# Attention, experts and FFN on one core: second product of expert blocks two and three from seven block products, interleaved with the first

## The chip, the cores and the metric

One core of one Trainium2 chip runs the whole program. The metric is the device time of one execution in microseconds (us). A product of matrices runs on TensorE (PE in the profile; PEld is its weight load), element-wise work on VectorE (DVE), ScalarE (ACT) and GpSimd (POOL); SyncE (SP) issues the DMAs. On-chip data lie in SBUF, TensorE's results in PSUM banks.

## What is computed

```python
x = attention(q, k, v)                 # 4 batches x 8 heads x 576 x 64, window 128, ALiBi -> x: 2304 x 512
P = exp(x @ w_gate - max); 8 x { P /= P.sum(1); P /= P.sum(0); P *= N / E }     # 2304 x 8
out = 0
for e in range(8):                     # experts, D = 512, F = 1024
    h = np.maximum(x @ w1[e], 0.0)     # "first product"
    out += P[:, e:e+1] * (h @ w2[e])   # "second product"
h = out @ w_in                         # FFN, 512 -> 2048
result = (h * np.cos(h)) @ w_out       # 2304 x 512
```

Everything is float32; a product of two float32 matrices is made of three products of parts (high x high, high x low, low x high).

## The kernel before

After the attention (the first 195 us) the tokens go through in three blocks of 768 (TB; half of it, HB, is 384, and TPB = 6 tiles of 128). Six phases follow each other: expert blocks ("moe", 0), ("moe", 1), ("moe", 2), which the text calls blocks one to three, then the same for the FFN. A phase runs over **units** of 256 hidden columns: NU1 = 32 units in an expert block (UPE = 4 for each expert), NU2 = 8 in an FFN block, 120 in all.

**First product of a unit** (`product`, L773). It is made from seven block products (a Strassen-Winograd scheme: 2 x 2 blocks with 7 products in place of 8), numbered m, each of six matmuls 128x384 (L766). Activations come from the seven tiles xtT../xtB.. that `stages` (POOL, L267) and `combos` (ACT L293, DVE L294) make once for a phase, weights from `wa` (1,792 KB). The main loop's order is `for m in (5, 1, 4, 2, 3, 6, 0, 7)`: product 4 is that of the unit before, and m = 0 stands for a **batch**. Products 1, 6, 7 and 4 add up in one PSUM bank y (two buffers), 5 and 3 in z, 2 in x; between them ACT copies the bank as it stands (`keep`, L796), and DVE adds copy and bank (L799). ReLU and the split into high and low part follow (ACT L722, DVE L723); in an FFN phase `cos_chain` (L732 to L755) does that, on ACT, DVE and POOL.

**Second product** (`batch`, `g2`, L870 to L872): 36 matmuls 128x512 for the unit before: six token tiles, each with two halves of the 256 columns and three part products. `evac` takes each of the six banks out on DVE and adds it, times the weight P of the token, to `acc_moe` (L861). Tokens are the rows of this sum. The FFN wants it the other way round, so ahead of each FFN phase `x2_pieces` turns it with 24 transposes on TensorE (L713), three to a step, and ACT copies (L716).

**Weights.** During block one the raw weights of a unit are loaded, the sums of the scheme (`prep_s`, POOL L120) and the split (`prep_a`: ACT L129, DVE L132; `prep_b`: ACT L143, POOL L145) are made, and the result is stored to HBM (wd1, wd2). Blocks two and three load it again: `wa` from wd1 with the load of unit n+1 issued behind product 4 of unit n-1 (L109, by SP), and `wb` (1,024 KB) from wd2 in the batch. Both have two buffers.

**Background.** `slot()` runs one step of each list of generators; slots lie between the products and in the batch. Among the generators is `convert_f64`: the FFN's weights come as 64-bit floats, and DVE converts them in 32 chunks of seven operations (L218 to L238), one chunk for a unit, in blocks two and three. `prep_ffn` (POOL L120 and L181, ACT L179) makes the sums and splits of the eight FFN units from them.

The order on each engine is the order of the code; each engine works off its own queue, and semaphores hold it where data is not there.

## Time and profile before

| what | value |
|---|---|
| median of three runs | 2098.69 us (2096.76 to 2104.01) |
| the profiled execution | 2100.89 us, of it span 2099.1 us |
| PE, DVE, ACT, POOL busy | 98%, 65%, 36%, 23% of the span |
| chain of work that ended last, by engine | PE 92%, DVE 4%, ACT 1%, issue 1% |
| DMA | 457 MB, mean 218 GB/s |

Busy time is the time in which an engine's instructions ran; the chain is followed back from the last instruction to what released it. Where PE is nearly always busy and nearly the whole chain, the length of PE's queue is the time, and the few gaps in it come on top. The page's rows stand further below.

### The profile page before, as it was taken

The numbers are of one execution on the slowest core, as the hardware profiler recorded it, in microseconds if no ns is written. First come the engines' busy times: TensorE is split into PE (matmuls) and PEld (weight loads), VectorE is DVE, ScalarE is ACT, GpSimd is POOL, SyncE is SP. The second block draws the span as 40 slices with busy tenths as digits, with TensorE's granted clock in tenths as the row PEclk, the third lists the DMA queues.
The fourth block names the chain that finished last, engine by engine and source line by source line (L and its number), as shares of the span: only waits on it lengthen the run. The fifth ranks groups of instructions, "written<-read, shape, count | busy, mean of one in ns | idle before, by whom it ended". The sixth has DMA issues, their size and how long they took to land.

```text
span 2099.1 us, 28328 instructions
## 1 busy us (share of the span) xinstructions
PE 2059.7 (98%) x10623; PEld 1821.5 (87%) x10623; DVE 1366.0 (65%) x2473; ACT 765.0 (36%) x1544; POOL 491.4 (23%) x524
## 2 busy tenths in 40 slices
PE   8989999999999999999999999999999999999998
PEld 6657889999899899899899899998998988899897
DVE  5665876666667677777776676555545565856765
ACT  6775433333333212222222322222221245454443
POOL 4343334333333002112113212110000113224222
PEclk9989999999999999999999999999999999999999
DMA  5633667767776568888888687675454454465552
GB/s 143 164 77 92 213 238 260 261 239 266 252 252 248 200 223 290 289 283 298 279 292 281 212 273 271 223 243 193 177 199 176 172 181 178 166 219 185 208 182 110
DMA packets 162106, 456.96 MB, mean 218 GB/s; under 512 B 67504, under 2 KB 106416, under 8 KB 131248
## 3 DMA queue, kind: packets, MB, share of 16 engines
q1 hardware_dynamic: 161968, 455.15, 63.2%
q8 instruction: 83, 1.36, 0.3%
q14 instruction: 55, 0.45, 0.1%
HBM read 326.65 MB, written 128.45 MB: 217 GB/s over the span
## 4 chain that ended last, share of the span: by engine, by line
PE 92%; DVE 4%; ACT 1%; issue 1%; POOL 0%; DMA 0%; POOLq 0%; DVEq 0%; ACTq 0%
PE y_moe L766 18%; PE g_moe L871 12%; PE g_moe L872 12%; PE g_moe L870 12%; PE z_moe L766 9%; PE x_moe L766 5%; PE y_ffn L766 4%; PE g_ffn L872 3%; PE g_ffn L870 3%; PE g_ffn L871 3%; PE s L443 3%; PE z_ffn L766 2%; PE x L535 2%; PE x_ffn L766 1%; PE T L407 1%
## 5 line engine op out<-in xcount | busy, mean ns | idle before, releaser
L861 DVE SCALAR_TENSOR_TENSOR acc_moe<-g_moe,prob,acc_moe 128x512 f32<-128x512 f32 x546 | 407.7, 748 | 142.3 <-PE g_moe L872 138.4
L870 PE MATMUL g_moe<-wb,h_moe 128*128 128x512 f32 x1152 | 450.8, 391 | 7.1 <-DVE acc_moe L861 7.1
L872 PE MATMUL g_moe<-wb,h_moe 128*128 128x512 f32 x1152 | 451.4, 392 | 0.0
L871 PE MATMUL g_moe<-wb,h_moe 128*128 128x512 f32 x1152 | 451.0, 391 | 0.0
L722 ACT ACTIVATE h_moe<-c_moe 128x768 fp32r<-128x768 f32 x192 | 131.9, 687 | 754.2 <-DVE c_moe L799 754.2
L766 PE MATMUL y_moe<-xtT_moe,wa 128*128 128x384 f32 x1728 | 348.7, 336 | 0.8 <-ACT s_moe L796 0.6
L766 PEld LDWEIGHTS y_moe<-xtT_moe,wa 128*128 128x128 f32 x1728 | 306.0, 188 | 8.7 <-ACT s_moe L796 0.9
L870 PEld LDWEIGHTS g_moe<-wb,h_moe 128*128 128x128 f32 x1152 | 217.1, 188 | 51.6 <-DVE acc_moe L861 9.0
L872 PEld LDWEIGHTS g_moe<-wb,h_moe 128*128 128x128 f32 x1152 | 216.8, 188 | 46.0 <-DVE h_moe L723 0.3
L871 PEld LDWEIGHTS g_moe<-wb,h_moe 128*128 128x128 f32 x1152 | 217.1, 188 | 43.1
L723 DVE SCALAR_TENSOR_TENSOR h_moe<-c_moe,h_moe 128x768 fp32r<-128x768 f32 x192 | 160.4, 836 | 59.9 <-ACT h_moe L722 59.9
L796 ACT ACTIVATE s_moe<-y_moe 128x384 f32<-128x384 f32 x192 | 94.4, 492 | 266.5 <-PE y_moe L766 266.3
L120 POOL TENSOR_TENSOR s<-ra 128x256 f32<-128x256 f32 x80 | 60.8, 760 | 504.1 <-DVE wa L132 291.0
L755 POOL TENSOR_TENSOR h_ffn<-c_ffn,h_ffn 128x768 fp32r<-128x768 f32 x48 | 92.7, 1949 | 314.1 <-ACT h_ffn L753 273.0
L799 DVE TENSOR_TENSOR c_moe<-z_moe,s_moe 128x384 f32<-128x384 f32 x96 | 53.4, 557 | 144.0 <-ACT s_moe L796 144.0
L723 DVE SCALAR_TENSOR_TENSOR h_moe<-y_moe,h_moe 128x384 fp32r<-128x384 f32 x96 | 53.5, 557 | 122.8 <-ACT h_moe L722 122.7
L766 PE MATMUL z_moe<-xtT_moe,wa 128*128 128x384 f32 x576 | 116.2, 335 | 2.0 <-DVE wa L132 1.9
L766 PE MATMUL y_moe<-xtB_moe,wa 128*128 128x384 f32 x576 | 115.6, 335 | 0.0
L766 PE MATMUL x_moe<-xtB_moe,wa 128*128 128x384 f32 x576 | 115.6, 335 | 0.0
L870 PE MATMUL g_ffn<-wb,h_ffn 128*128 128x512 f32 x288 | 113.1, 393 | 2.4 <-DVE acc_ffn L851 2.4
L766 PE MATMUL z_moe<-xtB_moe,wa 128*128 128x384 f32 x576 | 115.4, 334 | 0.0
L872 PE MATMUL g_ffn<-wb,h_ffn 128*128 128x512 f32 x288 | 112.8, 392 | 1.2 <-POOL h_ffn L755 1.2
(163 smaller groups left out, 3199.5 us busy)
## 6 DMA issues: line engine op xcount, KB each, us to landing
wa<-wd SPq DMA_DIRECT2D x88, 1792.0 KB, 8.1
wb<-wd SPq DMA_DIRECT2D x88, 1024.0 KB, 5.1
wd<-wa SPq DMA_DIRECT2D x32, 1792.0 KB, 6.7
wd<-wb SPq DMA_DIRECT2D x32, 1024.0 KB, 5.2
ra<-in_moe_w_dram SPq DMA_DIRECT2D x64, 256.0 KB, 7.3
rb<-in_moe_w_dram SPq DMA_DIRECT2D x64, 256.0 KB, 5.6
wd<-hla SPq DMA_DIRECT2D x48, 256.0 KB, 8.3
wd<-hlb SPq DMA_DIRECT2D x40, 256.0 KB, 8.8
```

The source lines that it names most:

```text
L120: nc.gpsimd.tensor_tensor(out=s4[:, o], in0=x, in1=y, op=op)
L443: nc.tensor.matmul(ps[:, x * 192 + c0:x * 192 + 192], qB[pi % 2][:, i, :], kT[pi][:, k0:k0 + w])
L722: nc.scalar.activation(out=h[:, 0, cols], in_=c, func=AF.Relu)
L723: low = lambda: nc.vector.scalar_tensor_tensor(out=h[:, 1, cols], in0=c, scalar=0.0, in1=h[:, 0, cols].bitcast(F32), op0=ALU.max, op1=ALU. ...
L755: nc.gpsimd.tensor_tensor(out=h[:, 1], in0=c, in1=h[:, 0].bitcast(F32), op=ALU.subtract)
L766: nc.tensor.matmul(ps[:, :HB], wa[:, wl, WI[m], kc, :], x[:, xl, kc, :], start=start and kc == 0 and n_ == 0, stop=stop and kc == 1 and n_ ...
L796: nc.scalar.activation(out=t["s", i], in_=ps[:, :HB], func=AF.Copy)
L799: nc.vector.tensor_tensor(out=o, in0=ps[:, :HB], in1=t["s", i], op=ALU.add)
L861: nc.vector.scalar_tensor_tensor(out=a, in0=ps, scalar=pe, in1=a, op0=ALU.mult, op1=ALU.add)
L870: nc.tensor.matmul(ps, hf[f][:, 0, ts], wb[:, 0, f, :], start=f == 0, stop=False)
L871: nc.tensor.matmul(ps, hf[f][:, 0, ts], wb[:, 1, f, :], start=False, stop=False)
L872: nc.tensor.matmul(ps, hf[f][:, 1, ts], wb[:, 0, f, :], start=False, stop=f == 1)
```

## The change

In expert blocks two and three the second product is also made from seven block products. The unit of work is a **pair** of units (512 hidden columns): 7 products, each in two halves d of the 512 output columns, so 14 **half-steps** (`s_step`) in a pair, each of six matmuls 128x384 (L976), in place of two batches of 36 matmuls 128x512.

- **Order.** `couple()` sets one half-step behind each first product, from the twelfth first product of block two on (the first matmul behind the eighteenth, in its third unit). The last 18 half-steps run in the first two units of the FFN, two to a first product.
- **Banks.** Four fixed banks gT; products 1, 6, 7, 4 add up in two of them (one for each d), 5 and 3, and then 2, in the other two. After each half-step DVE adds the bank to the accumulator (L988, 128x384; ACT L986 for the first of a block). The sum stands **transposed**: 512 columns on the partitions, tokens along the rows.
- **Operands.** ReLU is done in place by ACT (L890), and POOL multiplies h with the weights P (`weigh`, L887), of which a broadcast copy comes by DMA for each expert (`load_p`, L785). POOL also makes the four differences of h of a pair (L1009, 128x768). For each of the seven products ACT takes the high part (L1000, 128x768) and DVE the low part (L996, 128x768), and SP loads 512 KB of weights (L1004) into a ring of four.
- **Weights.** In block one `prep_sb` also makes the four sums of w2 of a unit (POOL, four 128x256), splits them (ACT L183, POOL L185, 128x1024) and stores them (wdp).
- **Transposes.** Only the accumulator of block one is turned for the FFN (`x2_piece`, six steps of four transposes, during block two); the second and third FFN phase read the transposed accumulators of expert blocks two and three as they are.
- **Background.** There are two more slots in a couple, a chunk of `convert_f64` starts only where no other is under way and not in every fourth unit (block two up to unit 25, block three from unit 1 on), and `prep_ffn` follows the chunks.

```diff
+        wbX = ring.tile([P, 4, 2 * DM], F32R, name="wbX")
+        SO = (1, 5, 3, 6, 7, 2, 4)
+        UPB = NU1 // 2
+        NPR = (NB - 1) * UPB
         wd1 = {u: dram.tile([P, 2 * 7 * 2 * P], F32, tag=f"wd1_{u}", name=f"wd1_{u}") for u in range(NU1 + NU2)}
-        wd2 = {u: dram.tile([P, 2 * 2 * DM], F32, tag=f"wd2_{u}", name=f"wd2_{u}") for u in range(NU1 + NU2)}
+        wd2 = {u: dram.tile([P, 2 * 2 * DM], F32, tag=f"wd2_{u}", name=f"wd2_{u}") for u in range(NU1, NU1 + NU2)}
+        wdp = {p: dram.tile([P, 7 * 2 * DM], F32, tag=f"wdp_{p}", name=f"wdp_{p}") for p in range(UPB)}
...
+        def prep_sb(u):
+            if not sb_t:
+                sb_t.append(blk.tile([P, 12, FU], F32, tag="k0", name="sb"))
+            sb = sb_t[0]
+            rb = raw_t[u, "b"]
+            raw, hl = sb[:, 0:4], sb[:, 4:12].bitcast(F32R).rearrange("p (o h) f -> p o h f", h=2)
+            a11, a12 = rb[:, 0, :FU], rb[:, 1, :FU]
+            a21, a22 = rb[:, 0, FU:], rb[:, 1, FU:]
+            for o, x, y, op in ((0, a21, a22, ALU.add), (2, raw[:, 0], a11, ALU.subtract),
+                                (3, a11, a21, ALU.subtract), (1, a12, raw[:, 2], ALU.subtract)):
+                nc.gpsimd.tensor_tensor(out=raw[:, o], in0=x, in1=y, op=op)
+                if o in (2, 1):
+                    yield
+            nc.scalar.activation(out=hl[:, :, 0], in_=raw, func=AF.Copy)
+            yield
+            nc.gpsimd.tensor_tensor(out=hl[:, :, 1], in0=raw, in1=hl[:, :, 0].bitcast(F32), op=ALU.subtract)
+            yield
+            yield
+            nc.sync.dma_start(out=pair_rows(u)[:, 1:5], in_=hl.bitcast(F32))
...
+        def x2_piece(tt):
+            a = accs["moe", 0][:, tt, :]
             for kc in range(KC):
-                for h in range(2):
-                    ps = p_m.tile([P, 512], F32, tag="m", name=f"x2_{b}_{kc}_{h}")
-                    for tt in range(GPB):
-                        nc.tensor.transpose(
-                            ps[:, tt * P:(tt + 1) * P], acc[:, h * GPB + tt, kc * P:(kc + 1) * P], ident
-                        )
-                    nc.scalar.activation(out=t[:, kc, h * HB:(h + 1) * HB], in_=ps[:, :HB], func=AF.Copy)
-                    yield
+                nc.tensor.transpose(gT[2][:, kc * P:(kc + 1) * P], a[:, kc * P:(kc + 1) * P], ident)
+            nc.scalar.activation(out=a, in_=gT[2], func=AF.Copy)
...
+        def load_p(g):
+            b, e = divmod(g, E)
+            if b >= NB - 1:
+                return
+            src = pT.rearrange("(i e) t -> e i t", e=E)[e, b * TPB:(b + 1) * TPB, :]
+            nc.sync.dma_start(out=Pb(g).rearrange("p (i t) -> p i t", t=P), in_=src.partition_broadcast(P))
...
+            if kind == "moe" and b:
+                x = u % 2
+                H = pair_t((b - 1) * UPB + u // 2)
+                pb = Pb((b - 1) * E + u // UPE).rearrange("p (a c) -> p a c", a=2)
+
+                def weigh(q, r):
+                    nc.gpsimd.tensor_tensor(out=H[:, q, x], in0=H[:, q, x], in1=pb[:, r], op=ALU.mult)
+
+                def relu(q, src):
+                    nc.scalar.activation(out=H[:, q, x], in_=src, func=AF.Relu)
+
+                if m == 5:
+                    keep(3, ps)
+                elif m == 1:
+                    keep(1, ps)
+                elif m == 2:
+                    add(H[:, 0, x], ps, 1)
+                elif m == 6:
+                    keep(2, ps)
+                    add(H[:, 1, x], t["z"], 2)
+                    both = slice(0, 2)
+                    defer(2, lambda: relu(both, H[:, both, x]))
+                    defer(3, lambda: weigh(both, both))
+                elif m == 7:
+                    add(H[:, 3, x], ps, 3)
+                    defer(2, lambda: relu(3, H[:, 3, x]))
+                    defer(3, lambda: weigh(3, 1))
+                elif m == 4:
+                    relu(2, ps[:, :HB])
+                    defer(2, lambda: weigh(2, 0))
+                    del st_t[s]
+                return
...
+        def pair_t(p):
+            if p % 2 == 0:
+                t = cX
+            else:
+                if not hodd:
+                    hodd.append(blk.tile([P, 2 * 2 * TB], F32, tag="k0", name="hodd"))
+                t = hodd[0]
+            return t.rearrange("p (q u c) -> p q u c", q=4, u=2)
+
+        OPQ = {1: 0, 5: 1, 3: 3, 6: 1, 7: 0, 2: 2, 4: 1}
+        CQ = {1: (0, 0), 2: (0, 0), 6: (0, 1), 3: (0, 1), 4: (1, 0), 7: (1, 1), 5: (1, 1)}
+        NK = 7 * NPR
+        sigma = [-6]
+
+        def op_slot(k):
+            o = k % 3 * 2 * TB
+            return hX[:, o:o + 2 * TB].rearrange("p (h u c) -> p h u c", h=2, u=2)
+
+        def s_step():
+            g = sigma[0]
+            sigma[0] += 1
+            k, d = g // 2, g % 2
+            if 0 <= k < NK:
+                pr, i = divmod(k, 7)
+                b, m = 1 + pr // UPB, SO[i]
+                w = wbX[:, k % 4].rearrange("p (u h f) -> p u h f", u=2, h=2)
+                x = op_slot(k)
+                ps = gT[d if m in (1, 6, 7, 4) else 2 + d]
+                seq = [(u, wl, 0) for u in range(2) for wl in range(2)] + [(u, 0, 1) for u in range(2)]
+                for n_, (u, wl, xl) in enumerate(seq):
+                    nc.tensor.matmul(
+                        ps[:, :HB], w[:, u, wl, d * P:(d + 1) * P], x[:, xl, u, :],
+                        start=m in (1, 5, 2) and n_ == 0, stop=m in (4, 3, 2) and n_ == 5,
+                        skip_group_check=True,
+                    )
+                if ("moe", b) not in accs:
+                    accs["moe", b] = blk_tile(acc_tag["moe", b], f"acc_moe{b}", [P, KC, TB])
+                r, c = CQ[m]
+                a = accs["moe", b][:, 2 * r + d, c * HB:(c + 1) * HB]
+                if pr % UPB == 0 and m in (1, 5, 3, 4):
+                    nc.scalar.activation(out=a, in_=ps[:, :HB], func=AF.Copy)
+                else:
+                    nc.vector.tensor_tensor(out=a, in0=ps[:, :HB], in1=a, op=ALU.add)
+                if i == 3 and d == 1 and 4 <= pr < 4 + TPB:
+                    x2_piece(pr - 4)
+            if d == 0:
+                k += 1
+                if 0 <= k < NK:
+                    x, H = op_slot(k), pair_t(k // 7)
+                    q = OPQ[SO[k % 7]]
+                    nc.vector.tensor_tensor(out=x[:, 1], in0=H[:, q], in1=x[:, 0].bitcast(F32), op=ALU.subtract)
+                return
+            if 0 <= k + 2 < NK:
+                x, H = op_slot(k + 2), pair_t((k + 2) // 7)
+                nc.scalar.activation(out=x[:, 0], in_=H[:, OPQ[SO[(k + 2) % 7]]], func=AF.Copy)
+            if 0 <= k + 3 < NK:
+                pr, i = divmod(k + 3, 7)
+                m, H = SO[i], pair_t(pr)
+                nc.sync.dma_start(
+                    out=wbX[:, (k + 3) % 4].bitcast(F32), in_=wdp[pr % UPB][:, i * 2 * DM:(i + 1) * 2 * DM]
+                )
+                t = {5: (1, 1, 0), 6: (1, 3, 1), 7: (0, 1, 0), 4: (1, 2, 1)}.get(m)
+                if t:
+                    nc.gpsimd.tensor_tensor(out=H[:, t[0]], in0=H[:, t[1]], in1=H[:, t[2]], op=ALU.subtract)
+            for j, kk in enumerate((NK - 3, NK - 1)):
+                if k == kk:
+                    load_w(NU1 + j, 0, "b")
+
+        LEAD = 14 + 4 - 6
+        couples = [0]
+
+        def couple():
+            for x in due:
+                x[0] -= 1
+            for x in [x for x in due if not x[0]]:
+                x[1]()
+            due[:] = [x for x in due if x[0]]
+            if couples[0] >= LEAD and sigma[0] < 2 * NK:
+                s_step()
+            couples[0] += 1
...
                 if nxt[0] == "ffn":
-                    feed.append(x2_pieces(nxt[1]))
-                    feed.append(lazy(lambda nxt=nxt: stages(nxt, x2r[nxt[1]])))
+                    feed.append(lazy(lambda nxt=nxt: stages(nxt, accs["moe", nxt[1]])))
                 else:
                     feed.append(stages(nxt, xr[nxt[1]]))
...
+                if new:
+                    couple()
+                    if kind == "ffn" and (u > NU1 or m in (2, 3, 6, 7)) and sigma[0] < 2 * NK:
+                        s_step()
+                    tick()
+                    slot()
...
-            queue.append(n)
-            if chunk < 4 * NU2 and ((kind, b) == ("moe", 1) and u < NU1 - 5 or (kind, b) == ("moe", 2)):
+            if kind == "ffn" or not b:
+                queue.append(n)
+            elif u % UPE == 0:
+                load_p((b - 1) * E + u // UPE + 1)
+            if chunk < 4 * NU2 and not bg and kind == "moe" and (b == 1 and u < NU1 - 6 or b == 2 and u > 0) and u % 4 != 3:
                 bg.append(convert_f64(chunk))
                 chunk += 1
-            at = n - NU1
-            if 0 < at <= 5 * NU2 and at % 5 == 0:
-                bg2.append(prep_ffn(NU1 + at // 5 - 1))
+            if ready < NU2 and 4 * (ready + 1) <= chunk - 1 + (not bg) and not bg2:
+                bg2.append(prep_ffn(NU1 + ready))
+                ready += 1
```

Two pieces of the scheduler show what stands in a row now. On PE, in the third expert block around unit 24: y, z and x are the banks of first products, g and gT those of second ones, h and hX the operands, wb and wbX the weights. Before:

```order
L766 MATMUL x_moe_24_14651<-xtB_moe_11552,wa_2_14533 128x384 x6
L766 MATMUL z_moe_24_14623<-xtB_moe_11566,wa_2_14533 128x384 x6
L766 MATMUL y_moe_24_14632<-xtT_moe_11636,wa_2_14533 128x384 x6
L870 MATMUL g_moe_23_0_14677<-wb_2_14494,h_moe_23_14559 128x512
L871 MATMUL g_moe_23_0_14677<-wb_2_14494,h_moe_23_14559 128x512
L872 MATMUL g_moe_23_0_14677<-wb_2_14494,h_moe_23_14559 128x512
```

The same place after, on PE:

```order
L840 MATMUL z_moe_24_14900<-xtT_moe_11524,wa_2_14822 128x384 x6
L976 MATMUL gT_2919<-hX,wbX 128x384 x6
L840 MATMUL y_moe_24_14919<-xtB_moe_11563,wa_2_14822 128x384 x6
L976 MATMUL gT_2920<-hX,wbX 128x384 x6
L840 MATMUL y_moe_23_14797<-xtT_moe_11675,wa_2_14699 128x384 x6
L976 MATMUL gT_2917<-hX,wbX 128x384 x6
L840 MATMUL x_moe_24_14956<-xtB_moe_11582,wa_2_14822 128x384 x6
L976 MATMUL gT_2918<-hX,wbX 128x384 x6
```

The batch of 36 behind product 6 is gone, and between any two first products there is one half-step of six matmuls.

On DVE, in the second expert block in unit 9, with the operations of one chunk (fa, fb) of the FFN's weights. Before:

```order
L799 TENSOR_TENSOR c_moe_9_8529<-x_moe_9_8522,s_moe_9_8506 128x384
L226 SCALAR_TENSOR_TENSOR fa_8495<-f_8_8457,fa_8495 128x512
L799 TENSOR_TENSOR c_moe_9_8529<-z_moe_9_8486,s_moe_9_8545 128x384
L861 SCALAR_TENSOR_TENSOR acc_moe_7484<-g_moe_8_0_8550,prob,acc_moe_7484 128x512
L723 SCALAR_TENSOR_TENSOR h_moe_9_8548<-c_moe_9_8529,h_moe_9_8548 128x768
L861 SCALAR_TENSOR_TENSOR acc_moe_7484<-g_moe_8_1_8559,prob,acc_moe_7484 128x512
L230 TENSOR_SCALAR fb_8496<-f_8_8457 128x512
```

The same place after, on DVE:

```order
L996 TENSOR_TENSOR hX<-hodd,hX 128x768
L988 TENSOR_TENSOR acc_moe_7473<-gT_2920,acc_moe_7473 128x384
L258 TENSOR_SCALAR fa_8369<-f_6_8153 128x512
L262 TENSOR_SCALAR fa_8369<-fa_8369 128x512
L988 TENSOR_TENSOR acc_moe_7473<-gT_2919,acc_moe_7473 128x384
L996 TENSOR_TENSOR hX<-hodd,hX 128x768
L264 TENSOR_SCALAR fa_8369<-fa_8369 128x512
L266 SCALAR_TENSOR_TENSOR fa_8369<-f_6_8153,fa_8369 128x512
```

The chunk's seven operations stood spread between the evacuations of the batch; now they stand close together, one or two in each slot, between the evacuations of half-steps and the low parts.

On SP, in the same block, from the load of `wa` of unit 9 on (wd is the store of prepared FFN weights, f the load of 64-bit weights, hX<-pT the broadcast of P). Before:

```order
L109 DMA wa_1_8378<-wd_9_96 128x3584
L175 DMA wd_32_119<-hlb_8219 256x1x256
L203 DMA f_8_8457<-in_moe_w_in_dram 128x512 x2
L175 DMA wd_32_119<-hla_8218 256x1x256
L109 DMA wb_1_8469<-wd_9_136 128x2048
L246 DMA w_7_8483<-fb_8356 128x512
```

The same place after, on SP:

```order
L119 DMA wa_1_8262<-wd_9_100 128x3584
L1004 DMA wbX<-wdp_142 128x1024
L215 DMA wd_32_123<-hlb_8061 256x1x256
L1004 DMA wbX<-wdp_142 128x1024
L215 DMA wd_32_123<-hla_8060 256x1x256
L785 DMA hX<-pT 128x6x128
L1004 DMA wbX<-wdp_142 128x1024
L215 DMA wd_32_131<-hlb_8061 128x2x256
```

One load of 1,024 KB became seven loads of 512 KB in two units, each issued at the end of a half-step.

## Rows read from the trace of the kernel before

**Rows 1.** Page, part 1: busy time, share of span, instructions.

```profile
PE 2059.7 (98%) x10623; PEld 1821.5 (87%) x10623; DVE 1366.0 (65%) x2473; ACT 765.0 (36%) x1544; POOL 491.4 (23%) x524
```

**Rows 2.** Page, part 4: the chain that ended last, by engine.

```profile
PE 92%; DVE 4%; ACT 1%; issue 1%; POOL 0%; DMA 0%; POOLq 0%; DVEq 0%; ACTq 0%
```

**Rows 3.** Timeline of PE, one unit of block three: start, duration, instruction.

```profile
1487.69 1.23 PE L766 MATMUL y_moe<-xtT_moe,wa 128*128 128x384 f32 x6
1488.76 1.20 PE L766 MATMUL z_moe<-xtT_moe,wa 128*128 128x384 f32 x6
...
1490.84 1.20 PE L766 MATMUL y_moe<-xtT_moe,wa 128*128 128x384 f32 x6
...
1495.00 0.39 PE L870 MATMUL g_moe<-wb,h_moe 128*128 128x512 f32 x1
...
1503.20 1.05 PE L766 MATMUL y_moe<-xtT_moe,wa 128*128 128x384 f32 x5
```

**Rows 4.** Timeline of PE, two steps of transposes ahead of the FFN.

```profile
1629.36 0.49 PE L713 MATMUL x<-ident,acc_moe 128*128 128x128 f32 x3
...
1630.74 0.49 PE L713 MATMUL x<-ident,acc_moe 128*128 128x128 f32 x3
```

**Rows 5.** Timeline of PE at the FFN's start; in brackets idle and releaser.

```profile
1701.12 1.31 PE L766 MATMUL y_ffn<-xtT_ffn,wa 128*128 128x384 f32 x6 [0.64 <-ACT s_ffn L796]
1704.69 2.26 PE L766 MATMUL z_ffn<-xtT_ffn,wa 128*128 128x384 f32 x6 [2.27 <-DMA wa<-wd]
...
1710.59 1.33 PE L766 MATMUL x_ffn<-xtB_ffn,wa 128*128 128x384 f32 x6
```

**Rows 6.** Windows: us, busy PE, PEld, DVE, ACT, POOL, clock, DMA share, GB/s.

```profile
1704.00:1711.00 7.00, 6.31 (x20) 6.34 (x21) 1.52 (x2) 1.97 (x4) 0.00 (x0) 0.51 0.00 0
...
206.00:690.00 484.00, 476.85 (x2387) 429.81 (x2386) 333.02 (x513) 181.96 (x310) 170.26 (x149) 1.00 0.70 244
800.00:1100.00 300.00, 300.00 (x1513) 272.30 (x1512) 228.83 (x368) 78.03 (x161) 50.21 (x56) 1.00 0.83 286
1410.00:1690.00 280.00, 279.52 (x1418) 253.05 (x1416) 146.15 (x217) 66.26 (x120) 7.61 (x4) 1.00 0.52 186
```

**Rows 7.** Groups by line and form: busy us, mean ns, idle before, releaser.

```profile
L799 DVE TENSOR_TENSOR c_moe<-z_moe,s_moe 128x384 f32<-128x384 f32 x96 | 53.4, 557 | 144.0 <-ACT s_moe L796 144.0
L749 DVE TENSOR_TENSOR c_ffn<-c_ffn,ta 128x768 f32<-128x768 f32 x48 | 43.9, 948 | 0.0
L753 ACT ACTIVATE h_ffn<-c_ffn 128x768 fp32r<-128x768 f32 x48 | 40.5, 843 | 4.0 <-DVE c_ffn L749 4.0
L145 POOL TENSOR_TENSOR wb<-rb,wb 128x1024 fp32r<-128x1024 f32 x32 | 77.4, 2419 | 18.1 <-ACT wb L143 18.1
L120 POOL TENSOR_TENSOR s<-ra 128x256 f32<-128x256 f32 x80 | 60.8, 760 | 504.1 <-DVE wa L132 291.0 <-DMA ra<-w 213.1
L238 DVE SCALAR_TENSOR_TENSOR fb<-fb,fa 128x512 f32<-128x512 f32 x32 | 21.7, 679 | 0.0
```

**Rows 8.** Line L755 alone: durations min/median/max in ns.

```profile
L755 POOL TENSOR_TENSOR h_ffn<-c_ffn,h_ffn x48: 1808/1847/2582, 1718.9 to 2086.1; 128x768 fp32r<-128x768 f32 x48
```

**Rows 9.** Line L294 alone: the same columns.

```profile
L294 DVE TENSOR_TENSOR xtT_ffn<-stT_ffn,xtT_ffn x12: 948/958/2384, 1681.2 to 1955.5; 128x768 fp32r<-128x768 f32 x12
```

**Rows 10.** Timeline of DVE and POOL at a change of FFN block.

```profile
1808.52 4.39 POOL L755 TENSOR_TENSOR h_ffn<-c_ffn,h_ffn 128x768 fp32r<-128x768 f32 x2 [11.91 <-ACT h_ffn L753]
1809.15 2.04 DVE L294 TENSOR_TENSOR xtT_ffn<-stT_ffn,xtT_ffn 128x768 fp32r<-128x768 f32 x1 [1.61 <-ACT xtT_ffn L293]
```

**Rows 11.** Tile wa, window 1410 to 1690.

```profile
DMA to landing us min/median/max: 7.0/7.2/8.4
```

**Rows 12.** Tile wa, window 780 to 1240.

```profile
DMA to landing us min/median/max: 7.2/8.9/10.8
```

**Rows 13.** Timeline of SP: issue of a load of wa.

```profile
1492.07 0.32 SPq L109 DMA_DIRECT2D wa<-wd  x1
```

**Rows 14.** DMA view, window 800 to 1100: GB/s in 40 slices.

```profile
GB/s 265 257 273 316 246 388 193 372 210 418 191 348 142 380 241 375 198 365 231 373 246 298 206 301 286 323 283 304 299 280 330 270 257 221 375 227 391 187 365 227
```

147 lines of the change are left out of this document (100 added, 47 removed).

## The prediction

> **What bounds the kernel now.** I read the page's busy times first, then the chain, then PE's timeline of one quiet unit, and only then the places where PE waits. PE is busy in 98% of the span [rows 1] and holds 92% of the chain [rows 2]; no other engine is above 65%. So the time is the length of PE's queue plus a few gaps. A unit in block three shows the length: from 1487.69 to the next unit's 1503.20 are 15.51 us; six product starts in a row, 1488.76 to 1495.00, are 6.24, so 1.04 for one product, and the batch takes 1495.00 to 1503.20 = 8.20 [rows 3]. The second product is thus over half of a unit, and DVE, ACT and DMA only have to be in time.
>
> **1. PE's work: -60.8.** A half-step has the form of a first product, six matmuls 128x384 with their own weights, so I price it at 1.04. A unit becomes 14 x 1.04 = 14.56 against 15.51: -0.95, and with 64 units -60.8. The order shows that this is really done: one half-step between any two first products, no batch.
>
> **2. Transposes: -6.** A product with three transposes ahead of it takes 1629.36 to 1630.74 = 1.38 [rows 4] in place of 1.04, so 0.34 a step and 8 x 0.34 = 2.7 for a phase. Two phases lose them (-5.4); some short waits on their copies go too (-0.6, my estimate). The six steps of block one's accumulator have as many transposes as its eight steps had: 0.
>
> **3. The FFN's start: -5.7.** There, PE waits 0.64 for a copy and 2.27 for `wa`, because with no batch in the first two units the load is not covered [rows 5]. Behind that the granted clock is 0.51 in the window 1704 to 1711, the lower level of 1.2 GHz, without a batch or transfer in it [rows 6], and three products take 1704.69 to 1710.59 = 5.90 in place of 3.12: 2.78 more. The 18 half-steps that now stand in those units fill the gap: -(0.64 + 2.27 + 2.78).
>
> **4. Block two's second unit: +6.5.** The same hole opens there. The first matmul of a half-step stands behind the eighteenth first product, so the second unit has neither batch nor half-steps. The load of `wa` is issued behind product 4 and needed four products later, 4 x 1.04 = 4.2 and the uncovered copy, 0.6, so 4.8 us, against landings of 7.0 to 8.4 [rows 11]: 2.2 to 3.6 of waiting, as long as the wait of [rows 5], and I add the same slow stretch of 2.8 and the 0.6: about 6.5. Ends: 3 (no slow stretch) and 10 (the next unit waits as well).
>
> **5. Block one: +2.** `prep_sb` adds four POOL sums of 128x256 at 0.76 to 1.0 (say 0.84) and a low part of 128x1024 at 2.42 [rows 7], 5.8 a unit, to POOL's 170.26 of 484 us [rows 6], 5.5 a unit: 11.3 of 15.5. It also stores 0.75 MB more. POOL still fits, but prepared weights may come later; I take +2, ends 0 and 10. The changes of block keep their waits: 0.
>
> **6. The covers in a quiet unit: 0.** What was hidden by 8.2 us of batch must now be hidden by half-steps. `keep` between products 6 and 7 needs 0.64 uncovered [rows 5] and has one half-step, 1.04. The load of `wa` is issued behind product 4 (1490.84 + 1.04 = 1491.88, issue at 1492.07 [rows 3, 13]) and is needed nine matmul groups later, 9 x 1.04 = 9.36, so it may take 9.1; it took 7.0 to 8.4 in block three [rows 11]. DVE has for a pair (29.1 us) 20 additions out of PSUM at 0.56 and seven low parts at 0.95 [rows 7], 17.8 us. ACT has seven high parts at 0.84 [rows 7] more, some 6 us, on a quarter of its time [rows 6]. POOL, new here, has four differences and two weightings of 128x768 at 1.85 [rows 8] and four weightings of 128x384, about 1.0 by the rows around it: 15.1. All fit, so in units without a chunk I see no wait: 64 x 0.
>
> **7. Units with a chunk: 32 x 0.8 = +25.6.** Here DVE gets tight. The seven 64-bit operations cost (228.83 / 300 - 146.15 / 280) x 15.51 = 3.7 us of DVE a unit, and `prep_ffn` 50.21 / 300 x 15.51 = 2.6 us of POOL [rows 6]. Before, they stood beside a batch of 8.2 us; now they stand in some four couples, 8.3 us, in which DVE's own work is 17.8 / 29.1 of that, 5.1: in all 8.8, a lag of 0.5. To this comes something that the row at a change of block shows: a DVE low part of 0.95 (median [rows 9]) took 2.04 while POOL ran [rows 10]; POOL's first operation ended at 1808.52 + 1.85 = 1810.37, and DVE's 0.82 later. It stood still until POOL was done, and only 0.13 of it ran beside. In those four couples DVE has two low parts and three 64-bit operations that read two operands in SBUF: five that can meet POOL. POOL is busy 52% (15.1 of 29.1) to 70% (with `prep_ffn`) of the time, and a meeting costs half of 1.85 - 0.13, so 0.86: 5 x 0.65 x 0.86 = 2.8. A bank may wait for its evacuation: the next half-step in it starts 2 x 2.08 - 1.04 = 3.1 after the last one's end, less the evacuation itself, 0.56: 2.5 of slack. So 0.5 + 2.8 - 2.5 = 0.8 us of PE waiting for a chunk unit. Ends: 0.2 (52%) and 2.0 (nearly every one of the five blocked). I take 0.8, since it goes by the row's own size; 32 chunks, one in a unit.
>
> [...]
>
> **Sum.** 2100.89 - 60.8 - 6 - 5.7 + 6.5 + 2 + 25.6 = 2062.5 for an execution like the profiled one, which lies 2.2 above the median of the runs: **2060**.
>
> **Rivals.**
>
> B, all is hidden: the chunk's operations find gaps, and term 7 is at most 0.2 x 32 = 6. Then 2060 - 25.6 + (0 to 6) = 2035 to 2041, with the ends of terms 4 and 5 some 2030 to 2045. For it: DVE has 39% of a pair free, and slack of 2.5. Against it: the long blockage in [rows 10].
>
> C, DVE and POOL become the bound: **slower**. If whatever reads two operands in SBUF excludes POOL in full, a chunk unit needs (15.1 + 6.65 of low parts) / 2 + 3.7 + 2.6 = 17.2 us of these two alone, in 14.56: 2.6 behind in each, which a later unit can't give back to PE. Then 2060 + 32 x (2.6 - 0.8) = 2118. It decides from 0.8 + 38.7 / 32 = 2.0 us a chunk unit on, where the gain of 38.7 is gone; at that size of a single gap the clock fell in [rows 5, 6], which would make it worse. Against it: only three of the seven 64-bit operations read two operands, one in four units has no new chunk, and 0.13 of each operation runs beside.
>
> D, `wa` comes late: the loop is product 4, issue, landing, and nine groups. In block two with chunks `wa` took 7.2 / 8.9 / 10.8 [rows 12], beyond the 9.1 of term 6 at its upper end; at 10.8 each chunk unit waits 1.7: 2035 + 32 x 1.7 = 2089, with the ends 2082 to 2098. For it: a unit now moves 1.8 MB of `wa`, 1.8 of ring (3.5 loads of 0.5), and in chunk units about 1.4 of 64-bit and FFN weights in less time, some 5.1 MB / 14.56 us = 350 GB/s, where the mean was 286 [rows 6]. Against it: slices of 7.5 us reached 391 and 418 [rows 14], and the ring spreads its loads. The Trainium skill, page "DMA: Bandwidth & Descriptors", section "Specifications", gives 358 GB/s from HBM for a core; by an estimate from that page 5.1 MB take 14.2 us, just within the unit. The slices above 358 in [rows 14] say that the measured limit is higher here.
>
> That the change doesn't do what it says is excluded by the order.
>
> **How the numbers follow.** A forecast with term 7 from 0.2 to 1.5 (2045 to 2082): 0.50. B: 0.20. D: 0.15. C: 0.12. Something else: 0.03. The predicted time is A's, 2060. The range reaches from 2036 (term 7 at 0.2, 2041, and term 5 or 4 at its low end) to 2098 (term 7 at 2.0, D's upper end); it leaves out C and the lower part of B. About 6 us, 0.3%, is what a measurement of this kernel tells from no change: faster means below 2092.4. A, B and two thirds of D lie there: 0.80. Within 0.3%: the rest of D and a little of C: 0.07. Slower: most of C and the unknown: 0.13.
>
> **What would show it.** Quiet unit of block three without a chunk: 14.56 from start to start, PE without gaps (terms 1, 6). Units with a chunk: PE waiting for DVE at L976, 0.2 to 1.5 a unit, with DVE low parts or 64-bit operations stretched beside POOL (term 7); if PE waits for the DMA of `wa` there, D; if nowhere, B. One gap near the second unit of block two and low clock behind it (term 4); none at the FFN's start (term 3). The prediction is wrong if half-steps take other than 1.04, or if quiet units wait too.

## The result, and the profile after

The changed kernel takes 2130.12 us in the median of four runs (2126.76 to 2135.60), the kernel before 2098.42 on the same chip: a ratio of 1.0149, 95% interval 1.0119 to 1.0179. Forecast were 2060 and a gain; it became 1.5% slower. The profiled execution took 2135.60 us, of it span 2133.7. In the profile after, the busy times and the chain stand against [rows 1, 2]; the columns are the same:

```profile
PE 2030.0 (95%) x10960; PEld 1862.1 (87%) x10960; DVE 1563.5 (73%) x2553; ACT 954.3 (45%) x1799; POOL 1233.0 (58%) x1004
...
PE 81%; DVE 11%; issue 3%; DMA 3%; ACT 2%; POOL 1%; SPq 0%; POOLq 0%; DVEq 0%; ACTq 0%
```

PE has less to do (2030 in place of 2060) and the time is longer: PE's share of the chain fell from 92% to 81%, DVE's rose from 4% to 11%. POOL's busy time went from 491 to 1233.

The work itself became as short as was expected. PE's timeline in a quiet part of block three shows two starts of product 5, one unit apart, and a half-step beside a first product:

```profile
1637.70 1.20 PE L976 MATMUL gT<-hX,wbX 128*128 128x384 f32 x6
1638.74 1.20 PE L840 MATMUL y_moe<-xtT_moe,wa 128*128 128x384 f32 x6
...
1649.14 1.20 PE L840 MATMUL z_moe<-xtT_moe,wa 128*128 128x384 f32 x6
...
1663.70 1.20 PE L840 MATMUL z_moe<-xtT_moe,wa 128*128 128x384 f32 x6
```

1663.70 - 1649.14 = 14.56 for a unit, against 15.51 in [rows 3], and 1.04 for a half-step. So the loss lies elsewhere. Measured from one phase's first start of product 5 to the next phase's, in PE's timeline (us):

| phase | before | after | difference | by the terms of the prediction |
|---|---|---|---|---|
| block one | 501.6 | 518.3 | +16.7 | +2 |
| block two | 500.3 | 512.5 | +12.2 | about -16 |
| block three | 499.9 | 498.3 | -1.6 | about -24 |
| first FFN block | 127.8 | 137.5 | +9.7 | about +1 |
| second FFN block | 129.0 | 126.0 | -3.0 | -3 |

(The 18 late half-steps move 18.7 us from block two to the first FFN block, which in turn has lost the last batch of block three, 8.2; the last column has both in it, and a chunk at 0.8 in 20 units of block two and 12 of block three.) The third FFN block is the same. Three places make up the 73 us between forecast and result: blocks two and three (+50), block one (+15), the FFN's start (+8).

The list of PE's waits over the whole program (us in total, times, longest) says on whom:

```profile
PE gT L976 <- issue: 29.8, 20, 2.6
PE z_moe L840 <- DMA wa<-wd: 8.8, 4, 7.2
...
PE gT L976 <- DVE acc_moe L988: 5.4, 10, 0.9
PE gT L976 <- ACT s_moe L869: 4.8, 5, 1.3
PE gT L976 <- DVE hX L996: 4.7, 8, 2.1
```

"issue" is a wait for which the profile shows no releaser. The timeline shows what it ends with: each of these 20 starts of L976 comes 0.10 us behind the end of a DVE evacuation L988, and so do the five that the list gives to ACT's s_moe. These are waits for a bank that DVE has not yet taken out. One of them in full, PE, DVE and POOL in block two:

```profile
826.60 1.20 PE L976 MATMUL gT<-hX,wbX 128*128 128x384 f32 x6
...
827.83 2.00 POOL L1009 TENSOR_TENSOR cX<-cX 128x768 f32<-128x768 f32 x1
828.19 2.19 DVE L274 SCALAR_TENSOR_TENSOR fb<-f,fb 128x512 f32<-128x512 uint32 x1
...
830.30 0.55 DVE L872 TENSOR_TENSOR hodd<-x_moe,s_moe 128x384 f32<-128x384 f32 x1
...
830.77 0.54 DVE L988 TENSOR_TENSOR acc_moe<-gT,acc_moe 128x384 f32<-128x384 f32 x1
...
831.41 2.04 PE L976 MATMUL gT<-hX,wbX 128*128 128x384 f32 x6 [2.58 <-issue]
```

Read it from below. PE waits 2.58 for the bank. The evacuation L988 ends at 831.31. It stood behind L872 and behind L274, one of the 64-bit operations, which takes 0.68 alone and took 2.19 here: it began while POOL's L1009 ran and ended at 830.38, 0.55 after POOL's end at 829.83. And behind the gap the half-step takes 2.04 and not 1.20: the granted clock is at its lower level for a while (0.57 in the window 831.4 to 833.4).

### The profile page after: what moved, and what is told of

The parts are those of the page before. It is cut to its first block, busy times and chain, and to the rows that moved or that the text cites. A ratio compares the mean times of both kernels' runs of the same rounds, so it can differ in the third digit from the quotient of the medians.

```text
span 2133.7 us, 30785 instructions
## 1 busy us (share of the span) xinstructions
PE 2030.0 (95%) x10960; PEld 1862.1 (87%) x10960; DVE 1563.5 (73%) x2553; ACT 954.3 (45%) x1799; POOL 1233.0 (58%) x1004
## 4 chain that ended last, share of the span: by engine, by line
PE 81%; DVE 11%; issue 3%; DMA 3%; ACT 2%; POOL 1%; SPq 0%; POOLq 0%; DVEq 0%; ACTq 0%
PE gT L976 19%; PE y_moe L840 16%; PE z_moe L840 8%; PE gT L1064 6%; PE gT L1062 6%; PE gT L1063 6%; PE y_ffn L840 4%; PE x_moe L840 4%; PE s L493 2%; PE z_ffn L840 2%; DMA wa<-wd 2%; PE x L585 2%; DVE hX L996 2%; PE x_ffn L840 1%; DVE acc_moe L988 1%
## 5 line engine op out<-in xcount | busy, mean ns | idle before, releaser
L976 PE MATMUL gT<-hX,wbX 128*128 128x384 f32 x2688 | 553.6, 340 | 47.1 <-issue 29.8
L976 PEld LDWEIGHTS gT<-hX,wbX 128*128 128x128 f32 x2688 | 474.0, 190 | 67.3 <-issue 35.7
L988 DVE TENSOR_TENSOR acc_moe<-gT,acc_moe 128x384 f32<-128x384 f32 x432 | 238.0, 552 | 152.8 <-PE gT L976 151.7
L1062 PE MATMUL gT<-wbX,hX 128*128 128x512 f32 x672 | 265.5, 395 | 12.6 <-DVE acc_moe L1053 5.5
L1064 PE MATMUL gT<-wbX,hX 128*128 128x512 f32 x672 | 265.5, 395 | 3.0 <-POOL hX L828 2.9
L1063 PE MATMUL gT<-wbX,hX 128*128 128x512 f32 x672 | 265.0, 394 | 0.0
L887 POOL TENSOR_TENSOR cX<-cX,hX 128x384 f32<-128x384 f32 (+1 forms) x96 | 140.0, 1462 | 93.4 <-ACT cX L890 78.1
L1009 POOL TENSOR_TENSOR cX<-cX 128x768 f32<-128x768 f32 x64 | 138.0, 2156 | 79.1 <-DVE hX L996 79.1
L887 POOL TENSOR_TENSOR hodd<-hodd,hX 128x384 f32<-128x384 f32 (+1 forms) x96 | 146.8, 1531 | 63.2 <-ACT hodd L890 63.2
L1009 POOL TENSOR_TENSOR hodd<-hodd 128x768 f32<-128x768 f32 x64 | 140.4, 2194 | 50.9 <-DVE hX L996 50.9
L1062 PEld LDWEIGHTS gT<-wbX,hX 128*128 128x128 f32 x672 | 127.9, 190 | 40.1 <-DVE acc_moe L1053 5.9
L1064 PEld LDWEIGHTS gT<-wbX,hX 128*128 128x128 f32 x672 | 127.6, 190 | 31.3 <-POOL hX L828 3.7
L1063 PEld LDWEIGHTS gT<-wbX,hX 128*128 128x128 f32 x672 | 127.9, 190 | 25.6
L996 DVE TENSOR_TENSOR hX<-hodd,hX 128x768 fp32r<-128x768 f32 x112 | 139.7, 1248 | 0.8 <-ACT hX L1000 0.8
L996 DVE TENSOR_TENSOR hX<-cX,hX 128x768 fp32r<-128x768 f32 x112 | 136.8, 1221 | 2.2 <-ACT hX L1000 2.2
```

The costliest lines, as they stand in the source:

```text
L887: nc.gpsimd.tensor_tensor(out=H[:, q, x], in0=H[:, q, x], in1=pb[:, r], op=ALU.mult)
L976: nc.tensor.matmul(ps[:, :HB], w[:, u, wl, d * P:(d + 1) * P], x[:, xl, u, :], start=m in (1, 5, 2) and n_ == 0, stop=m in (4, 3, 2) and n ...
L988: nc.vector.tensor_tensor(out=a, in0=ps[:, :HB], in1=a, op=ALU.add)
L996: nc.vector.tensor_tensor(out=x[:, 1], in0=H[:, q], in1=x[:, 0].bitcast(F32), op=ALU.subtract)
L1009: nc.gpsimd.tensor_tensor(out=H[:, t[0]], in0=H[:, t[1]], in1=H[:, t[2]], op=ALU.subtract)
L1062: nc.tensor.matmul(ps, hf[f][:, 0, ts], wb[:, f, 0, :], start=f == 0, stop=False)
```

## The experiments

All kernels start from the changed one, except one that starts from the kernel before. A time given alone is that of one execution; the four of the changed kernel lie within 9 us. It is compared with the kernel before on the same chip (one execution, 2100.09, for the runs without the chunks' operations, without POOL's new work, with one operation for each half-step and without the sums of w2). In the expectations, T is the theory that DVE and POOL exclude each other and DVE comes late.

**Without the chunks' DVE operations.**

```diff
-            nc.vector.tensor_scalar(
-                out=a, in0=hi, scalar1=20, scalar2=0x7FF, op0=ALU.logical_shift_right, op1=ALU.bitwise_and
-            )
...
+            nc.scalar.activation(out=w, in_=hi.bitcast(F32), func=AF.Copy)
```

> The seven DVE operations of each of the 32 chunks are left out; one ACT copy of 128x512 stands in their place, loads, stores and prep_ffn stay. Theory T (the 64-bit operations and POOL's new operations exclude each other, DVE falls behind, PE waits some 2.35 us in each chunk unit, 32 x 2.35 = 75): units of blocks two and three at 14.56, time about 2055 (2045 to 2068). Rival R1 (the operations' own DVE time, 4.3 us a chunk, and their place ahead of the evacuations is enough for the wait): the same 2055. Rival R2 (the wait comes from the transfers or from ACT in those units): about 2130, units stay near 17.

2067.81. Block two fell from 512.5 to 475.0, block three from 498.3 to 472.4, and 55 of the 60 units behind the hole and the change of block stand at 14.56 to 15.1. The transfers of those units were unchanged, so R2 falls; T and R1 remain. Block one (514.7) and the first FFN block (138.6) hardly moved: their losses have other causes.

**Without POOL's new work.**

```diff
-                    nc.gpsimd.tensor_tensor(out=H[:, q, x], in0=H[:, q, x], in1=pb[:, r], op=ALU.mult)
+                    pass
...
-                if t:
-                    nc.gpsimd.tensor_tensor(out=H[:, t[0]], in0=H[:, t[1]], in1=H[:, t[2]], op=ALU.subtract)
```

> POOL's weighting of h and its four differences of a pair are left out (15 us of POOL in 29), the 64-bit operations and prep_ffn stay. T: the 64-bit operations fall back to their lone 0.42 and 0.68 us, the low parts to 0.95, chunk units to at most 14.9, time 2055 to 2068. R1: the operations get shorter or not, but the units stay at 16 or more, since 4.3 us of DVE and their place are unchanged: 2100 to 2130. R2: no change, 2130.

2061.92: blocks two and three at 473.3 and 467.8, although every one of the 64-bit operations is there, at its old place. So R1 falls: DVE's own time and the order are harmless without POOL. The groups by line and form (busy us, mean ns) show what POOL had done to them. The changed kernel:

```profile
L258 DVE TENSOR_SCALAR fa<-f 128x512 int32<-128x512 int32 x32 | 48.4, 1513 | 9.8 <-DMA f<-in_moe_w_in_dram 7.8 <-DMA f<-in_moe_w_out_dram 2.0
L262 DVE TENSOR_SCALAR fa<-fa 128x512 int32<-128x512 int32 x32 | 41.7, 1303 | 1.1
L266 DVE SCALAR_TENSOR_TENSOR fa<-f,fa 128x512 int32<-128x512 int32 x32 | 43.5, 1359 | 1.1
L278 DVE SCALAR_TENSOR_TENSOR fb<-fb,fa 128x512 f32<-128x512 f32 x32 | 21.8, 681 | 0.0
L996 DVE TENSOR_TENSOR hX<-cX,hX 128x768 fp32r<-128x768 f32 x112 | 136.8, 1221 | 2.2 <-ACT hX L1000 2.2
L988 DVE TENSOR_TENSOR acc_moe<-gT,acc_moe 128x384 f32<-128x384 f32 x432 | 238.0, 552 | 152.8 <-PE gT L976 151.7
```

The one without POOL's new work:

```profile
L258 DVE TENSOR_SCALAR fa<-f 128x512 int32<-128x512 int32 x32 | 13.4, 420 | 11.7 <-DMA f<-in_moe_w_in_dram 9.3 <-DMA f<-in_moe_w_out_dram 2.3
L262 DVE TENSOR_SCALAR fa<-fa 128x512 int32<-128x512 int32 x32 | 14.6, 457 | 1.1
L266 DVE SCALAR_TENSOR_TENSOR fa<-f,fa 128x512 int32<-128x512 int32 x32 | 22.7, 708 | 1.1
L996 DVE TENSOR_TENSOR hX<-cX,hX 128x768 fp32r<-128x768 f32 x112 | 113.2, 1011 | 2.9 <-ACT hX L1000 2.8
L988 DVE TENSOR_TENSOR acc_moe<-gT,acc_moe 128x384 f32<-128x384 f32 x432 | 239.5, 555 | 208.5 <-PE gT L976 207.0
```

L258, L262 and L266 shrink to a third or a half, the first two of them operations with a single operand; the other 64-bit operations shrink by less, and the last of a chunk, L278, took 0.68 in the changed kernel already. The evacuation, which reads PSUM and one operand in SBUF, is the same (552 and 555). The FFN's first block fell too, from 137.5 to 133.1.

**The kernel before, with POOL work added.** The same cost by itself, in the other kernel:

```diff
                 tick()
+                if kind == "moe" and b and 2 <= u < 27 and m in (5, 4, 3, 7):
+                    y = xr[b]
+                    nc.gpsimd.tensor_tensor(out=y[:, 0], in0=y[:, 0], in1=y[:, 1], op=ALU.subtract)
```

> The kernel before, with four POOL operations 128x768 of two operands in SBUF added to each of units 2 to 26 of blocks two and three, on data that nobody reads (as much POOL time as the change brings: 7.4 us a unit). T: the 64-bit operations stretch from 0.42 and 0.68 to means of 0.9 to 1.4 us, the low parts of 0.95 to 1.2, while operations that read PSUM keep 0.56 and 0.74; PE is covered by the batch in most units, so 2100 to 2125. Rival (the stretch in the changed kernel comes from its transfers or its order, not from POOL): the durations stay at 0.42, 0.68 and 0.95, time 2100.

2128.86 against 2099.47, 27.6 of it in block two (527.9 in place of 500.3), where 27 of the 32 chunks run; block three, with the same POOL work and five chunks, is 2.0 longer. Groups of block two, window 740 to 1140:

```profile
L861 DVE SCALAR_TENSOR_TENSOR acc_moe<-g_moe,prob,acc_moe 128x512 f32<-128x512 f32 x148 | 108.0, 740 | 5.3 <-PE g_moe L872 4.8
L234 DVE SCALAR_TENSOR_TENSOR fb<-f,fb 128x512 f32<-128x512 uint32 x25 | 38.5, 1541 | 0.0
L230 DVE TENSOR_SCALAR fb<-f 128x512 int32<-128x512 int32 x25 | 24.2, 968 | 0.0
L224 DVE TENSOR_SCALAR fa<-fa 128x512 int32<-128x512 int32 x25 | 21.2, 850 | 0.0
```

Without any half-step, ring or new order, the 64-bit operations stretch, those of two operands from 0.68 to 1.4 to 1.54, those of one from 0.42 to 0.56 to 0.97, and L861 out of PSUM stays at 0.74. So POOL's operations are what stretches them (the lock, as the text calls it), and the kernel before pays for it as well. T's price was slightly low (2125 at most), and the low parts of 128x768 (L723), for which it had 1.2, took 1.02.

**One operation of a chunk for each half-step.** The whole computation, with the seven operations spread:

```diff
-        def slot():
+        def slot(conv=True):
...
-            step_all(bg)
+            if conv:
+                step_all(bg)
...
                     tick()
+                    if not bg and chunk < 4 * NU2 and kind == "moe" and u < NU1 - 6 and (b == 1 or u > 0):
+                        bg.append(convert_f64(chunk))
+                        chunk += 1
                     slot()
                 if m not in (3, 6):
-                    slot()
+                    slot(not new)
```

> The whole computation; a chunk steps only once behind each half-step, not in a second slot, so its seven operations spread over some ten couples, and the next chunk starts where the last ended (fewer rests between). T: a couple of 2.08 us holds 1.27 of DVE's own work and one operation of 0.4 to 2.2, so the lag no longer adds up; 50 units with 0.3 to 0.7 of waiting: 2075 to 2095. R1: DVE's own time fits now, waits vanish: about 2060. R2: no change, 2130.

2086.31, in T's range, and now faster than the kernel before. Block two 484.0, block three 480.5. The seven operations together are as long as before (7.6 us a chunk, 7.5 in the changed kernel); only the lag no longer adds up ahead of an evacuation.

**Without the sums of w2.**

```diff
-            for m, f, o in ((1, 0, 0), (2, 1, 0), (4, 1, FU)):
+            for m, f, o in ((1, 0, 0), (2, 1, 0), (4, 1, FU), (5, 0, 0), (3, 0, FU), (6, 1, 0), (7, 1, FU)):
...
-                nc.gpsimd.tensor_tensor(out=raw[:, o], in0=x, in1=y, op=op)
...
-            nc.scalar.activation(out=hl[:, :, 0], in_=raw, func=AF.Copy)
...
-            nc.gpsimd.tensor_tensor(out=hl[:, :, 1], in0=raw, in1=hl[:, :, 0].bitcast(F32), op=ALU.subtract)
```

> In block one the sums of w2 (four POOL sums, ACT copy, POOL low part) are left out; the same bytes are stored from the split weights. Theory S (block one's 16.7 us more come from these operations: the ACT copy of the sums stands in ACT's queue until the store before has left the tile, ReLU stands behind it): block one from 518 back to about 503, time about 2116. Rival (they come from the moved Sinkhorn bank, the transposed weights P or the fixed h tiles): block one stays at 515 or more, time about 2130.

2116.54, block one at 503.5: its loss is these operations, and with them gone what is left is 1.9 over the kernel before.

**Block one's start and the hole in block two's second unit.** From here on each kernel includes the spread chunks.

```diff
+            if u == 2:
+                for _ in range(5):
+                    yield
             if not sb_t:
...
+            if 7 < couples[0] <= 7 + TPB:
+                x2_piece(couples[0] - 8)
```

> The whole computation: the kernel with one operation per couple, and three small moves: the sums of w2 of unit 2 begin five slots later (so that ACT's copy no longer stands waiting for the store before), two slots lie between Sinkhorn and the transposes of P, and block one's accumulator is turned in block two's second unit, where PE waits for wa, not later. Theory S: unit 2 of block one falls from 24.8 to about 17, the transposes' 1.4 goes, the hole of 6.9 shortens by 2: 2086 - 11 = about 2075 (2068 to 2080). Rival: the wait only moves to the next copy in unit 3 and the hole is set by the landing alone (its end stays): 2083 to 2087.

2084.52 (2083.01 to 2087.61), ratio 0.9926 [0.9903, 0.9950]. The rival held: unit 2 fell from 24.8 to 17.1, but unit 3 rose from 18.1 to 24.0 on waits for DVE's `wa` and the accumulator, and ACT's copy of its sums now stood 6.7 for the store, as that of unit 2 had stood 7.6. The wait for `wa` in the hole shortened from 6.9 to 5.2, but units 1 and 2 of block two, with the transposes in them, grew from 27.5 to 29.0: the end of the wait is set by the landing.

**Weighing one part of h straight out of PSUM.**

```diff
-                    relu(2, ps[:, :HB])
-                    defer(2, lambda: weigh(2, 0))
+                    nc.vector.scalar_tensor_tensor(
+                        out=H[:, 2, x], in0=ps[:, :HB], scalar=0.0, in1=pb[:, 0], op0=ALU.max, op1=ALU.mult
+                    )
```

> As the kernel with the three small moves, and of the four parts of h the one of product 4 gets ReLU and weight in a single DVE operation that reads PSUM and one operand in SBUF; an ACT ReLU and a POOL weighting of 128x384 go (1.3 us of POOL a unit), DVE gets 0.56. T (what counts is what reads SBUF twice on DVE beside POOL): less contention, the remaining 25 us of waits in blocks two and three fall by 5 to 12: about 2065. Rival R3 (DVE's load counts, 64% becoming 68%, whatever it reads): same or slower by 2 to 8: 2075 to 2083.

2079.26 (2076.77 to 2080.59), ratio 0.9896 [0.9869, 0.9923]. DVE has more to do and the kernel gets 5 us faster than with the three small moves; blocks two and three fell from 484.9 and 485.0 to 479.0 and 479.4. The time itself lies in R3's range, but both ranges counted from the 2075 expected for the moves, which came out at 2084.52. Counted from there the change of -5.3 speaks for T, at the low end of its gain, and against R3, which had no gain (the two intervals overlap a little). POOL also has less to do here, so the run doesn't separate that from the place of the operand.

**The raw load of w2 earlier.**

```diff
+            yield
+            if u + 2 < NU1:
+                load_raw(u + 2, "b")
             nc.scalar.activation(out=hl[:, :, 0], in_=raw, func=AF.Copy)
...
             nc.sync.dma_start(out=pair_rows(u)[:, 1:5], in_=hl.bitcast(F32))
-            if u + 2 < NU1:
-                load_raw(u + 2, "b")
```

> As the kernel that weighs product 4's part out of PSUM, but without the delay of unit 2's sums; instead the load of the raw w2 of two units later is issued behind the four sums, ahead of ACT's copy and the store. Theory S2 (block one's start is late because the loads of raw weights stand behind the new work, and later units wait for them): units 2 to 5 of block one fall from 17.1 + 24.0 + 18.8 + 17.2 = 77 to about 70, time 2072. Rival S (ACT's copy of the sums standing behind the store of the sums before is the cause): unit 2 is back at 24 to 25, time 2079 to 2082.

2076.60 (2071.83 to 2079.86), ratio 0.9886 [0.9866, 0.9907]. Units 2 to 5 of block one took 73.5, in place of 79.5 with the chunks spread alone and 77.1 with the sums delayed (the kernel before: 67.5); unit 2 alone 18.1, not 24, though the delay was taken out again. ACT's copy of unit 2's sums, which had stood idle 7.52 for the store of the sums before, stood 0.99. S2 is nearer than S, but the wait that S names went with the same change, so the run doesn't separate the two; half of the loss at block one's start stays open.

**POOL's long operations in halves.** The differences, and likewise the joint weighting of two parts of h:

```diff
-                    nc.gpsimd.tensor_tensor(out=H[:, t[0]], in0=H[:, t[1]], in1=H[:, t[2]], op=ALU.subtract)
+                    for z in range(2):
+                        nc.gpsimd.tensor_tensor(out=H[:, t[0], z], in0=H[:, t[1], z], in1=H[:, t[2], z], op=ALU.subtract)
```

> As the kernel that weighs product 4's part out of PSUM, with POOL's differences and the joint weighting of 128x768 each made as two of 128x384 (same work, 1.0 in place of 1.85 to 2.2 us for one). T (a DVE operation with the shared operand waits until the POOL operation that runs has ended): the longest blockage halves, DVE's low parts and 64-bit operations get shorter in the mean, waits in blocks two and three fall by 3 to 8 us: 2071 to 2076. Rival (the lock is passed over only when both have nothing queued, or POOL's extra overhead counts as much): no gain, 2078 to 2085.

2077.55 (2071.98 to 2080.48), ratio 0.9882 [0.9862, 0.9902]: between the two, and not to be told from 2079 by its time. Its waits say more. PE's waits from 740 to 1720, and the landings of `wa` from 740 to 1700:

```profile
PE z_moe L846 <- DMA wa<-wd: 9.4, 7, 2.8
PE gT L987 <- DVE hX L1005: 2.1, 5, 0.8
PE gT L1076 <- POOL hX L834: 1.7, 1, 1.7
```

```profile
DMA to landing us min/median/max: 6.9/7.4/12.1
```

The waits for banks are gone but for one of 0.4, and the most of what is left in blocks two and three behind the hole are seven waits for `wa` of up to 2.8, the wait of rival D. Against the kernel that it starts from, waits for DVE and ACT there fell from 9.8 to 2.3 and those for `wa` rose from 4.3 to 9.4: the two blocks stand at 477.6 and 479.3, hardly less than 479.0 and 479.4, and T's gain of 3 to 8 us there did not come. The first FFN block fell from 138.7 to 133.2.

**Both.**

> The raw load of w2 ahead of the copy and POOL's 128x768 operations in halves, together. T and S2 are independent (one acts in block one's first units, the other in blocks two and three and at the FFN's start): block one 511, FFN block one 133, together 2072 to 2075. Rival (their gains were spread between executions, not effects): 2077 as each alone.

2065.88 (2062.75 to 2068.10) against 2099.66, ratio 0.9840 [0.9826, 0.9853]: better than expected, and the fastest of those that compute the whole result, 1.6% under the kernel before and 3% under the changed one. Block one is at 510.8 and the first FFN block at 133.8, as expected; blocks two and three are at 474.6 and 475.1, some 4 us less each than with either change alone, which was not expected and which no run explains.

## Why the prediction was wrong

The range ended at 2098, and a slower kernel had a chance of 0.13. The largest part of the miss is term 7.

**Term 1 (PE's work) and term 6 (quiet units): right.** 14.56 a unit and 1.04 a half-step, as forecast; 24 of the 30 units without a chunk behind the hole and the change of block stand there, the others at up to 15.92. POOL's new operations took 17.7 a pair, not 15.1. Without POOL's new work block three takes 467.8, and 32 x 14.56 are 465.9.

**Term 2 (transposes): right.** The second FFN block is 3.0 shorter; 2.7 and a short wait were forecast.

**Term 7 (units with a chunk): wrong, and with it the sign of the result.** 25.6 us were forecast. The 30 units with a chunk behind the hole lie 70.4 us above their 14.56 each: 2.35 for a chunk (0.8 to 4.6), some 75 for all 32, beyond the 2.0 from which rival C was said to decide. The step that failed is the count of what can meet POOL: "two low parts and three 64-bit operations that read two operands in SBUF: five". The four with one operand were taken as free, and they are the ones that met POOL most: they went from 0.42 to means of 0.78 to 1.51 in the changed kernel, and to 0.56 to 0.97 in the kernel before with POOL work. One of them in the changed kernel:

```profile
824.11 1.46 POOL L221 TENSOR_TENSOR hlb<-ra,hlb 128x256 fp32r<-128x256 f32 x1
824.89 0.96 DVE L264 TENSOR_SCALAR fa<-fa 128x512 int32<-128x512 int32 x1
```

It ends at 825.85, 0.28 after POOL's end at 825.57. So do, of the 128 one-operand operations in the changed kernel's trace, all the 95 that took over 0.1 longer than alone; the 36 stretched ones of the 96 with two operands end 0.55 after a POOL operation, and the 100 stretched low parts (L996) 0.81 after one, each within 0.02. That is the time alone less some 0.14, as in [rows 10], where it was 0.82 for 0.95. A stretched 64-bit operation lost 0.9, so the price of a meeting, 0.86, was right. A chunk has 3.0 such meetings with one operand and 1.1 with two, and its two low parts lost 0.2 together: 3.9 us in place of 2.8. In the same working 0.5 + 3.9 - 2.5 = 1.9, an estimate made after the result; the lower clock (below) adds some 0.4, against the 2.35 measured.

A row of the kernel before tells of it (line L218 alone, ns min/median/max):

```profile
L218 DVE TENSOR_SCALAR fa<-f x32: 419/420/965, 711.2 to 1273.5; 128x512 int32<-128x512 int32 x32
```

0.42 for 512 columns, where L238 with two operands took 0.68 [rows 7], and a longest one of 0.965. The Trainium skill, page "SBUF — State Buffer", section "Who interferes with whom", states that `tensor_scalar` can enter the two-port modes and can then contend with GpSimd. The trace agrees (L258: 420 ns without POOL's new work, 1513 in the mean beside it). The prediction counted by the number of operands alone.

A second part was named under rival C but not priced in this term: behind five of the eight gaps of 1.8 to 2.6 us in block two the granted clock fell to its lower level, as in [rows 5, 6]. Between 755 and 1194 the product starts lie 40 us further apart than at full pace; 28.7 of it are waits (24.8 of idle time, and the overlap with the product before, which a wait takes away), 7.4 are products at the lower clock, some 0.4 for each of the 18 units with a chunk there, and most of the rest are block one's transposes.

**Term 5 (block one): mis-sized, +15 to +17 in place of +2, ends 0 to 10.** POOL's busy time fitted, as was said, and from unit 6 on units do stand at 15.51, but for unit 29 and the last (3.3 more in all). The first six units are 13.4 longer than in the kernel before. In the longest of them, ACT's copy of the sums stands first in ACT's queue and waits, and ReLU stands behind it. In the changed kernel:

```profile
230.45 1.06 ACT L183 ACTIVATE sb<-sb 128x1024 fp32r<-128x1024 f32 x1 [7.52 <-DMA wdp<-sb]
...
231.94 0.80 PE L1062 MATMUL gT<-wbX,hX 128*128 128x512 f32 x1 [4.08 <-ACT hX L790]
```

The term priced busy time and not what is queued behind a waiting instruction. The runs show that the work for the sums is the cause (503.5 without it) and that an earlier raw load gives a part back; which of the waits for store, load and DVE's low parts holds the rest is not settled.

**Term 3 (the FFN's start): wrong sign.** The wait for `wa` and the slow stretch behind it did go, but others came: the first FFN block is 8 longer than by the terms. In the changed kernel there:

```profile
1726.70 2.54 POOL L1009 TENSOR_TENSOR hodd<-hodd 128x768 f32<-128x768 f32 x1
...
1727.94 2.10 DVE L996 TENSOR_TENSOR hX<-cX,hX 128x768 fp32r<-128x768 f32 x1
...
1730.10 0.62 PE L976 MATMUL gT<-hX,wbX 128*128 128x384 f32 x2 [2.10 <-DVE hX L996]
```

A low part of 0.95 took 2.10 beside POOL, and in the same queue stood the low parts of the new block's activations. It is the same lock: without POOL's new work, and with it in halves, this block takes 133.1 and 133.2. That is about half of the 8; waits of 0.6 to 1.7 on ACT and POOL in the FFN's first units stay in those runs too. The prediction had named the gain there and not what is late next.

**Term 4 (the hole): right place, mis-sized.** Block two's second unit takes 15.51 where its seven products need 7.3: 8.2 more, and the products behind it lose 2.0 at the lower clock: 10.2, just past the upper end of 10, forecast 6.5. The wait alone was 7.15 in place of 2.2 to 3.6, because this load of `wa` landed after 12.1 us, not 7.0 to 8.4; loads of 64-bit weights, of the ring and of P were under way with it. The slow stretch was 2.0, not 2.8:

```profile
742.14 2.26 PE L840 MATMUL z_moe<-xtT_moe,wa 128*128 128x384 f32 x6 [7.15 <-DMA wa<-wd]
```

**The rivals.** B (all hidden) fell. D did not decide: behind the hole PE waited for `wa` no more than 0.24 in any unit with a chunk; it is what comes next once DVE is in time. C, with a chance of 0.12, was right in its place and its sign, and in that DVE and POOL exclude each other. It too counted only what reads two operands, and it took the sum over a whole unit, where the spread chunks show that it matters how close the operations stand. That its 2118 comes near the 2130 is partly luck: some 23 us of the result come from block one and the FFN's start, where C had no more than the forecast.

## What to carry to other kernels

Before work is given to an idle engine, list which operations of its neighbour can be held up by it, the fast one-operand operations included (0.42 for 512 columns here, against 0.68 with two), and price each meeting by the rest of the operation that runs: an engine busy 73% of the time, as DVE was here, may be late if a few of its instructions stand still for 2 us ahead of the one that the bottleneck waits for. Then the cheap cures are the order (one foreign operation between two evacuations), shorter operations on the other engine, and, less clearly, reading out of PSUM: here they, with an earlier load in block one, turned 1.5% slower into 1.6% faster without touching the new arithmetic. And price a new instruction not by its duration alone, but by what stands behind it in its queue while it waits.
